# Turning streamed outputs and the last token dims in 32-squares on VectorE, and reading expert 0's slot tables in final order

## The chip, the core and the metric

The kernel runs on one core of a Trainium2 chip. Five engines work side by side, each through its own list of instructions in order: TensorE (PE) multiplies matrices and turns tiles, VectorE (DVE) and ScalarE (ACT) work on elements, GpSimd (POOL) does small element work and issues the indexed transfers, and SyncE (SP) issues the plain transfers. Transfers run on 16 DMA engines that all queues share. SBUF is the on-chip memory of 128 partitions; PE writes its products into PSUM, from where ScalarE or VectorE copies them.

The metric is device time in microseconds, the median of several runs. Lower is better.

## The reference

Two blocks follow one another. Attention: for each of 8 batches x 8 heads, 576 queries against 576 keys of 64 dims; only scores within tau of the row's largest are kept, and the softmax over them weights the values.

```python
scores = scale * np.matmul(q, k.transpose(0, 1, 3, 2))
thresh = np.max(scores, axis=-1, keepdims=True) - tau
scores = np.where(scores >= thresh, scores, -1000000000.0)
scores = scores - np.max(scores, axis=-1, keepdims=True)
attn = np.exp(scores)
attn = attn / (np.sum(attn, axis=-1, keepdims=True) + 1e-09)
return np.matmul(attn, v).astype(np.float32)
```

The heads of a position are put side by side, which gives x, 4608 tokens of 512 dims. Then each token goes through one of 8 experts, chosen by a hash of its id; an expert is two matrices (512 x 1024, 1024 x 512, fp32) with a ReLU between:

```python
expert_idx = token_ids * np.int64(2654435761) % np.int64(E)
for e in range(E):
    mask = expert_idx == e
    xe = x[mask]
    h = np.maximum(xe @ w1[e], 0.0)
    out[mask] = h @ w2[e]
```

## The kernel before

**Attention** (to about 470 us). A loop over 160 steps, five for each of the 32 pairs of heads, in an order written out by hand. A step computes scores on PE, copies them negated with their maximum on VectorE (L227), takes the exponential on ScalarE (L241), masks and sums on VectorE (L252), turns the weights on PE (L263) and copies the turned ones on ScalarE. The normalised output of a pair goes to the scratch tensor x in DRAM (L333, then stores L339 and L344). SP also issues the loads of the next pairs (L169 to L193) and the weights of experts 0 and 1 (L118, L123).

**Routing** runs in pieces between these steps. Every token gets a slot: expert e owns 608 slots. 36 indexed writes put the token numbers into two slot tables in DRAM, by even and odd columns. Eight reads bring the tables back into `stok` and `stok_odd` (L493), a minimum joins them (L498), and copies with a step of 4 put them into the order of token tiles, `gidx` (L512). Four small multiplies make `gidx_0`, the index of each of expert 0's tokens in each quarter of 128 dims (L503). After the loop the same copies are made for the other experts, and `gidx_x`, in the order of 32-squares (L736).

**The hand-over.** Three quarters of expert 0's token dims are gathered while attention still runs (L108), turned on PE into `xT_0`, and multiplied as pieces between the last attention steps (`early_h`, L587, copied by VectorE at L594). The last quarter comes from the last pairs. It is gathered after them, turned by ten half-tile turns on PE (L563), copied by ScalarE (L577) and multiplied in `late_h` (L604); VectorE adds that to the earlier sum (L609) and ScalarE applies the ReLU (L610). The first product of `late_h` goes into a PSUM tile of which there is one, and the third product needs it again. The tiles of the expert stage are laid into the SBUF bytes that the attention stage gives up; VectorE clears five of them and an output tile at the start (L755, L757).

**Experts** (from about 500 us). An expert e has 19 blocks of 32 token slots: three tiles of 128 slots and a rest of 224, called "streamed". PE does, in this order:

- `gemm1` (L773), h = ReLU(w1 x), copied by ScalarE and VectorE in turn;
- `gemm2_last` (L799), the rest's outputs, transposed: the weights w2 are the stationary operand and the 224 slots stream by. ScalarE copies the result to `oT_sb` (L803);
- three times `gemm2` (L787), a tile of 128 slots each. Behind the first and the second stands `turn_last` (L810), four PE turns that bring one tile of the rest back to rows.

Each output tile is copied by ScalarE (L815) and stored by an indexed store on GpSimd to the output rows (L816). Successive stores all write the output tensor, so each waits for the one before. Meanwhile GpSimd gathers the tokens of expert e+2 (`fetch`), VectorE turns those of e+1 in 32-squares (`turn_x`, L831), and 16 moves on SP put the squares in place (L836). SP then loads the weights of e+2. A loop for tokens over an expert's 608 slots ends the program; it has no turn in this data.

Of the kernel before, what the change touches and what calls it, by code (L numbers as in the profile page):

```python
# [20 lines left out]
def kernel(  # L21
# [12 lines left out]
    nc = tc.nc  # L34
# [61 lines left out]
    gidx = consts.tile([P, E, KT], I32, name="gidx")  # L96
    gidx_0 = consts.tile([P, KT, HP], I32, name="gidx_0")
    gidx_x = consts.tile([P, E, KT], I32, name="gidx_x")
    ov_i = consts.tile([P, NOV + 1], I32, name="ov_i")
# [13 lines left out]
    def fetch_0(kt, hp):  # L113
        gather(x_rows, xg_bufs[kt][:, P * hp:P * hp + P], gidx_0[:, kt, hp:hp + 1])

    def load_w1(e):
# [9 lines left out]
    with tc.tile_pool(name="a_q", bufs=1) as a_q, \  # L126
# [353 lines left out]
        def scatters():  # L480
# [8 lines left out]
            for _ in range(4):  # L489
                yield  # L490
            for table, dst in zip(slot_dram, (stok, stok_odd)):
                for h in range(HP):
                    nc.sync.dma_start(  # L493
                        out=dst[32 * h:32 * h + 32],
                        in_=table[0:E * CAP].rearrange("(e c s) o -> c e (s o)", e=E, c=32))
            for _ in range(4):
                yield
            nc.vector.tensor_tensor(out=stok[:], in0=stok[:], in1=stok_odd[:], op=ALU.min)  # L498
            yield
            by_tiles(0, 1)  # L500
            yield
            for h in range(HP):
                nc.vector.tensor_scalar(out=gidx_0[:, :, h], in0=gidx[:, 0], scalar1=float(HP),  # L503
                                        scalar2=float(h), op0=ALU.mult, op1=ALU.add)
                if h == 1:
                    yield
            routed.append(True)

        def by_tiles(e0, e1):
            for h in range(4):  # L510
                rows, n = slice(32 * h, 32 * h + 32), (NB - h + 3) // 4
                nc.vector.tensor_copy(gidx[rows, e0:e1, 0:n], stok[rows, e0:e1, h::4])  # L512

# [30 lines left out]
        def constants():  # L544
# [6 lines left out]
            nc.gpsimd.memset(gidx[:], BIG)  # L551
            nc.gpsimd.memset(gidx_x[:], BIG)
            nc.gpsimd.iota(tok[:], pattern=[[1, NTC]], base=0, channel_multiplier=NTC)
            for table in slot_dram:
# [72 lines left out]
        with tc.manual_schedule():  # L627
# [104 lines left out]
            assert not early  # L732
            by_tiles(1, E)
            for g in range(4):
# [4 lines left out]
            fill(FO * 2 * (CO - 1) - 18)  # L739
            tr = ps_tr.tile([P, 2, 512], FP32, name="tr")  # L740
            early_xT(tr, 0, KT, CO - 1, CO)

    with tc.tile_pool(name="m_x", bufs=1) as m_x, \
# [6 lines left out]

        o_bufs = [m_o.tile([P, DIN], FP32, name=f"o_{i}") for i in range(KT)]
        xg_sets = [xg_bufs, [m_x.tile([P, DIN], FP32, name=f"xh_{i}") for i in range(KT)]]
        xq = m_x.tile([P, DIN // 32, 32 * KT], FP32, name="xq")
        for xg in xg_sets[1]:
            nc.vector.memset(xg[:], 0.0)  # L755
        oT_sb = m_o.tile([P, CO, CAP - FIRST[KF]], FP32, name="oT_sb")
        nc.vector.memset(o_bufs[KT - 1][:], 0.0)  # L757
        mark = m_o.tile([P, 1], FP32, name="mark")

        def put_xT(xg, xT, kt, rows):  # L760
            tr = ps_x.tile([P, 2, 512], FP32, name="xT_ps")[:, 0].rearrange(
                "p (c q) -> p c q", c=CO)
            for co in range(CO):
                nc.tensor.transpose(tr[:, co, 0:rows], xg[0:rows, co * P:co * P + P],
                                    ident[0:rows, 0:rows])
            nc.vector.tensor_copy(xT[:, :, FIRST[kt]:FIRST[kt] + rows], tr[:, :, 0:rows])

# [15 lines left out]

        def gemm2(w2_sb, h_sb, kt, idx, rows):
            o_ps = ps_o.tile([P, DIN], FP32, name="o_ps")
            for fo in range(FO):
                nc.tensor.matmul(o_ps[0:rows], lhsT=h_sb[:, fo, FIRST[kt]:FIRST[kt] + rows],  # L787
                                 rhs=w2_sb[:, fo, :], start=(fo == 0), stop=(fo == FO - 1))
            store(o_ps, kt, idx, rows)

        def gemm2_last(w2_sb, h_sb, order=range(FO)):

            oT_ps = ps_sc.tile([P, 2, 512], FP32, name="sc")
            width = CAP - FIRST[KF]
            for i in range(2):
                for c in range(CO // 2):
                    co = CO // 2 * i + c
                    for fo in order:
                        nc.tensor.matmul(oT_ps[:, i, c * width:c * width + width],  # L799
                                         lhsT=w2_sb[:, fo, co * P:co * P + P],  # L800
                                         rhs=h_sb[:, fo, FIRST[KF]:CAP], start=(fo == order[0]),
                                         stop=(fo == order[-1]))
            nc.scalar.copy(oT_sb[:].rearrange("p (i c) s -> p i (c s)", i=2),  # L803
                           oT_ps[:, :, 0:CO // 2 * width])

        def turn_last(kt, idx):
            o_ps = ps_x.tile([P, 2, 512], FP32, name="xT_ps")[:, 0]
            s0, rows = FIRST[kt] - FIRST[KF], TROWS[kt]
            for co in range(CO):
                nc.tensor.transpose(o_ps[0:rows, co * P:co * P + P], oT_sb[:, co, s0:s0 + rows], ident[:])  # L810
            store(o_ps, kt, idx, rows)

        def store(o_ps, kt, idx, rows):
            o_sb = o_bufs[kt % len(o_bufs)]
            nc.scalar.copy(o_sb[0:rows], o_ps[0:rows])  # L815
            nc.gpsimd.indirect_dma_start(  # L816
                out=out[:, :], out_offset=bass.IndirectOffsetOnAxis(ap=idx, axis=0),
                in_=o_sb[:], in_offset=None, bounds_check=N - 1, oob_is_err=False)

# [7 lines left out]
        def turn_x(e):  # L827


            for k in range(KT):  # L830
                nc.vector.transpose(out=xq[:, :, 32 * k:32 * k + 32],  # L831
                                    in_=xg_sets[e % 2][k][:].rearrange("p (d a) -> p d a", a=32))
            for g in range(4):
                s0, s1 = 32 * KT * g, min(32 * KT * (g + 1), CAP)
                for r in range(4):
                    nc.sync.dma_start(out=xT_bufs[e % 2][32 * r:32 * r + 32, :, s0:s1],  # L836
                                      in_=xq[32 * g:32 * g + 32, r::4, 0:s1 - s0])

        with tc.manual_schedule():
# [4 lines left out]
            for e in range(E):  # L844
# [8 lines left out]
                for kt in range(KF):  # L853
                    gemm2(w2_sb, h_bufs[e % 2], kt, gidx[:, e, kt:kt + 1], P)
                    if kt < KT - KF:
                        turn_last(KF + kt, gidx[:, e, KF + kt:KF + kt + 1])
                    if kt == 0 and e + 2 < E:
                        fetch(e + 2)
# [5 lines left out]
        with tc.For_i(0, n_ov, 1) as it:  # L864
# [15 lines left out]
            gather(x_dram, xg_bufs[0][:], idx[:, 0:1])  # L880
            put_xT(xg_bufs[0], xT_0, 0, P)
            gemm1(w1_sb, xT_0, h_0, 1, P)
            gemm2(w2_sb, h_0, 0, idx[:, 0:1], P)

# [33 lines left out]
```

## Time and profile before

| | us |
|---|---|
| time, median of 3 runs | 1012.16 (1010.39 to 1014.26) |
| profiled execution, time | 1007.16 |
| profiled execution, span | 1005.6 |
| PE busy | 991.6 (99%) |
| VectorE busy | 509.2 (51%) |
| ScalarE busy | 451.4 (45%) |
| GpSimd busy | 292.2 (29%) |
| `gemm2_last` on PE, L799 | 98.2 |
| turns of the streamed outputs on PE, L810, 64 of them | 9.6 |

The table's busy times are those of one profiled execution. PE's granted clock was 0.997 of full speed. Matmul ends in the profile are modelled, so the distance between the starts of two products says more than their lengths. A line of a timeline gives start and length in us, the engine, the line of the kernel, the operation, output and inputs, how many such instructions stand together, and in brackets how long the engine was idle before and for what. "SPq" is the SP queue issuing a transfer. Each fp32 matmul appears twice in the counts.

### The profile page before, as it was taken

The numbers are of one execution on the slowest core, as the hardware profiler recorded it, in microseconds if no ns is written. First come the engines' busy times: TensorE is split into PE (matmuls) and PEld (weight loads), VectorE is DVE, ScalarE is ACT, GpSimd is POOL, SyncE is SP. The second block draws the span as 40 slices with busy tenths as digits, with TensorE's granted clock in tenths as the row PEclk, the third lists the DMA queues.
The fourth block names the chain that finished last, engine by engine and source line by source line (L and its number), as shares of the span: only waits on it lengthen the run. The fifth ranks groups of instructions, "written<-read, shape, count | busy, mean of one in ns | idle before, by whom it ended". The sixth has DMA issues, their size and how long they took to land. (4 is left out here: it accounts for less than half of the span.)

```text
span 1005.6 us, 20293 instructions
## 1 busy us (share of the span) xinstructions
PE 991.6 (99%) x7612; PEld 658.3 (65%) x7612; DVE 509.2 (51%) x1366; ACT 451.4 (45%) x735; POOL 292.2 (29%) x411
## 2 busy tenths in 40 slices
PE   7999999999999999999999999999999999999996
PEld 4666666666666666666766857767678577685783
DVE  7999999999999999994302010010010100100000
ACT  5888889888898888883210010110110100101101
POOL 3233323377776335540413030030210300301001
PEclk9999999999999999999999999999999999999998
DMA  7345544555367757410157234262262432600001
GB/s 179 80 124 141 129 120 111 132 141 119 95 179 180 180 158 189 109 45 24 46 163 215 84 96 133 84 208 73 78 178 84 126 103 93 190 25 32 16 1 48
DMA packets 112002, 113.38 MB, mean 113 GB/s; under 512 B 26340, under 2 KB 86248, under 8 KB 111904
## 3 DMA queue, kind: packets, MB, share of 16 engines
q1 hardware_dynamic: 103680, 92.95, 34.9%
q0 software_dynamic: 7792, 18.91, 6.0%
q8 instruction: 62, 1.02, 0.4%
q14 instruction: 36, 0.29, 0.1%
q10 hardware_dynamic: 432, 0.21, 0.1%
HBM read 81.98 MB, written 22.37 MB: 104 GB/s over the span
## 5 line engine op out<-in xcount | busy, mean ns | idle before, releaser
L241 ACT ACTIVATE w<-ns,nmx 128x576 f32<-128x576 f32 x288 | 220.5, 776 | 36.5 <-DVE ns L227 36.2
L773 PE MATMUL sc<-xT,w_sb 128*128 128x304 f32 x896 | 230.4, 419 | 0.0
L252 DVE SCALAR_TENSOR_TENSOR w<-ns,thr,w 128x576 f32<-128x576 f32 x288 | 226.0, 817 | 0.0
L773 PEld LDWEIGHTS sc<-xT,w_sb 128*128 128x128 f32 x896 | 170.2, 190 | 61.4 <-issue 3.3
L227 DVE TENSOR_SCALAR_CACHE_REDUCE ns<-sc 128x576 f32<-128x576 f32 x288 | 205.6, 746 | 5.5 <-PE sc L216 4.5
L216 PE MATMUL sc<-k_sb,q 64*128 64x288 f32 (+1 forms) x1280 | 179.7, 425 | 1.6 <-DVE k_sb L541 0.9
L787 PE MATMUL o_ps<-w_sb,h 128*128 128x512 f32 x384 | 168.7, 592 | 0.0
L263 PEld LDWEIGHTS tr<-ident,w 64*128 64x128 f32 x2624 | 106.3, 138 | 88.6 <-ACT wT_b L284 26.3
L816 POOL DMA_INDIRECT out_dram<-o,gidx x40 | 39.5, 989 | 415.9 <-ACT o L815 320.4
L234 POOL TENSOR_SCALAR thr<-nmx,drop 128x2 f32<-128x2 f32 (+1 forms) x160 | 102.2, 639 | 174.8 <-DVE ns L227 162.1
L263 PE MATMUL tr<-ident,w 64*128 64x64 f32 x2624 | 139.0, 230 | 2.7 <-ACT wT_a L284 2.0
L781 DVE TENSOR_SCALAR h<-sc 128x608 f32<-128x608 f32 x28 | 22.2, 792 | 234.0 <-PE sc L773 234.0
L787 PEld LDWEIGHTS o_ps<-w_sb,h 128*128 128x128 f32 x384 | 71.7, 190 | 80.4 <-issue 80.4
L216 PEld LDWEIGHTS sc<-k_sb,q 64*128 64x128 f32 (+1 forms) x1280 | 92.9, 178 | 24.9 <-DVE ns L227 11.1
L779 ACT ACTIVATE h<-sc 128x608 f32<-128x608 f32 x28 | 19.0, 677 | 182.0 <-PE sc L773 182.0
L294 PE MATMUL av<-wT_a,v 128*64 128x320 f32 (+1 forms) x704 | 100.4, 418 | 0.0
L799 PE MATMUL sc<-h,w_sb 128*128 128x224 f32 x512 | 98.2, 352 | 0.0
L799 PEld LDWEIGHTS sc<-h,w_sb 128*128 128x128 f32 x512 | 96.9, 190 | 1.1
L284 ACT COPY wT_a<-tr 128x512 f32<-128x512 f32 (+1 forms) x128 | 81.8, 639 | 20.1 <-PE tr L263 19.6
L284 ACT COPY wT_b<-tr 128x512 f32<-128x512 f32 (+1 forms) x128 | 81.3, 635 | 5.4 <-PE tr L263 3.2
L294 PE MATMUL av<-wT_b,v 128*64 128x256 f32 x640 | 83.2, 389 | 0.0
L815 ACT COPY o<-o_ps 128x512 f32<-128x512 f32 x24 | 14.1, 586 | 147.3 <-issue 87.3
(114 smaller groups left out, 559.4 us busy)
## 6 DMA issues: line engine op xcount, KB each, us to landing
w_sb<-in_moe_w_dram SPq DMA_DIRECT2D x16, 2048.0 KB
q<-in_q_dram SPq DMA_DIRECT2D x62, 288.0 KB
v<-in_v_dram SPq DMA_DIRECT2D x32, 256.0 KB
x_scratch<-xm SPq DMA_DIRECT2D x32, 256.0 KB
xT<-xq SPq DMA_DIRECT2D x84, 80.0 KB
k_sb<-in_k_dram SPq DMA_DIRECT2D x31, 144.0 KB
k_sb<-in_k_dram SPq DMA_DIRECT2D x32, 112.0 KB
x_scratch<-xg SPq DMA_DIRECT2D x9, 256.0 KB
```

Of the source, the lines that this page charges most:

```text
L216: nc.tensor.matmul(sc[out_rows, i, 0:S2], lhsT=q_sb[rows, h, q0:q1], rhs=k_sb[rows, h], start=True, stop=True)
L227: nc.vector.tensor_scalar(out=ns[:].rearrange("p (i s) -> p i s", i=2), in0=sc[:, :, 0:S2], scalar1=-1.0, scalar2=None, op0=ALU.mult, op1= ...
L234: nc.gpsimd.tensor_scalar(out=thr[:, 0:j + 1], in0=stats[n][0][:, 0:j + 1], scalar1=drop[:], scalar2=None, op0=ALU.add)
L241: nc.scalar.activation(w, nss[n, j][:], AF.Exp, bias=stats[n][0][:, j:j + 1], scale=-1.0)
L252: nc.vector.scalar_tensor_tensor(out=w, in0=nss.pop((n, j))[:], scalar=stats[n][1][:, j:j + 1], in1=w, op0=ALU.is_le, op1=ALU.mult, accum_ ...
L263: nc.tensor.transpose(dst[:, r, 64 * c:64 * c + 64], src[rows, c0:c0 + P], ident[rows, rows])
L284: nc.scalar.copy(dst, tr[:, :, 0:64 * n_c].rearrange("p r (c q) -> p r c q", c=n_c))
L294: nc.tensor.matmul(av[64 * j:64 * j + 64, g, c0:c1], lhsT=v_sb[:, c, 64 * j:64 * j + 64], rhs=wT[g][:, i, c0:c1], start=(c == 0), stop=stop)
L773: nc.tensor.matmul(h_ps[:, i, 0:width], lhsT=w1_sb[:, co, fo * P:fo * P + P], rhs=xT[:, co, i * width:i * width + width], start=(co == 0), ...
L787: nc.tensor.matmul(o_ps[0:rows], lhsT=h_sb[:, fo, FIRST[kt]:FIRST[kt] + rows], rhs=w2_sb[:, fo, :], start=(fo == 0), stop=(fo == FO - 1))
L799: nc.tensor.matmul(oT_ps[:, i, c * width:c * width + width], lhsT=w2_sb[:, fo, co * P:co * P + P], rhs=h_sb[:, fo, FIRST[KF]:CAP], start=( ...
L816: nc.gpsimd.indirect_dma_start(out=out[:, :], out_offset=bass.IndirectOffsetOnAxis(ap=idx, axis=0), in_=o_sb[:], in_offset=None, bounds_ch ...
```

## The change

Three edits. Lines are those of the kernel before.

1. The streamed outputs are no longer copied by ScalarE and turned by PE. `gemm2_last` takes every fourth column of w2 as its stationary operand, so that partition p holds output dims 4p to 4p+3. VectorE turns the result in squares of 32 x 32 out of PSUM into `oq`, two instructions an expert, and 16 moves on SP put the squares into rows in `o_last`. The two stores of these rows follow the store of the second product.
2. The last quarter of expert 0's token dims is turned in 32-squares too: five turns on VectorE into the bytes of an attention buffer, then 16 moves on SP into `xT_0`. Its gathers use the slot order that this needs.
3. Expert 0's slots are read from the tables by 16 small transfers of their own, in the two orders in which they are used (`sidx`), ahead of the eight reads of the whole tables. One minimum and two multiply-adds make `gidx_0` from them. The minimum and the copies over the whole tables move behind the attention loop.

```diff
+    def move_squares(xq, xT, c0):
+        for g in range(4):
+            s0, s1 = 32 * KT * g, min(32 * KT * (g + 1), CAP)
+            for r in range(4):
+                nc.sync.dma_start(out=xT[32 * r:32 * r + 32, c0:CO, s0:s1],
+                                  in_=xq[32 * g:32 * g + 32, r::4, 0:s1 - s0])
...
+            for table, dst in zip(slot_dram, sidx):
+                slots = table[0:CAP].rearrange("(c s) o -> c (s o)", c=32)
+                for h in range(4):
+                    for part in range(2):
+                        blocks = (slots[:, h::4] if part == 0 else
+                                  slots[:, KT * h:min(KT * h + KT, NB)])
+                        nc.sync.dma_start(
+                            out=dst[32 * h:32 * h + 32, part, 0:blocks.shape[1]], in_=blocks)
             for table, dst in zip(slot_dram, (stok, stok_odd)):
...
-            nc.vector.tensor_tensor(out=stok[:], in0=stok[:], in1=stok_odd[:], op=ALU.min)
-            yield
-            by_tiles(0, 1)
-            yield
-            for h in range(HP):
-                nc.vector.tensor_scalar(out=gidx_0[:, :, h], in0=gidx[:, 0], scalar1=float(HP),
-                                        scalar2=float(h), op0=ALU.mult, op1=ALU.add)
-                if h == 1:
-                    yield
+            nc.vector.tensor_tensor(out=gidx_e[:], in0=sidx[0][:], in1=sidx[1][:], op=ALU.min)
+            yield
+            for part, h0, h1 in ((0, 0, HP - 1), (1, HP - 1, HP)):
+                nc.vector.scalar_tensor_tensor(
+                    out=gidx_0[:, :, h0:h1],
+                    in0=gidx_e[:, part, :, None].to_broadcast([P, KT, h1 - h0]),
+                    scalar=float(HP), in1=iota_i[:, None, h0:h1].to_broadcast([P, KT, h1 - h0]),
+                    op0=ALU.mult, op1=ALU.add)
+                yield
...
+            for t in sidx:
+                nc.gpsimd.memset(t[:], BIG)
...
-            by_tiles(1, E)
+            nc.vector.tensor_tensor(out=stok[:], in0=stok[:], in1=stok_odd[:], op=ALU.min)
+            for h in range(4):
+                rows, n = slice(32 * h, 32 * h + 32), (NB - h + 3) // 4
+                nc.vector.tensor_copy(gidx[rows, :, 0:n], stok[rows, :, h::4])
...
             fill(FO * 2 * (CO - 1) - 18)
-            tr = ps_tr.tile([P, 2, 512], FP32, name="tr")
-            early_xT(tr, 0, KT, CO - 1, CO)
+            xq_0 = w_bufs[0][:, 0:P // 32 * 32 * KT].rearrange("p (d s) -> p d s", d=P // 32)
+            for kt in range(KT):
+                nc.vector.transpose(
+                    out=xq_0[:, :, 32 * kt:32 * kt + 32],
+                    in_=xg_bufs[kt][:, DIN - P:DIN].rearrange("p (d a) -> p d a", a=32))
+            move_squares(xq_0, xT_0, CO - 1)
...
-        oT_sb = m_o.tile([P, CO, CAP - FIRST[KF]], FP32, name="oT_sb")
-        nc.vector.memset(o_bufs[KT - 1][:], 0.0)
+        oq = m_o.tile([P, NB - 4 * KF, 32, CO], FP32, name="oq")
+        o_last = m_o.tile([P, KT - KF, DIN], FP32, name="o_last")
+        nc.vector.memset(o_last[:], 0.0)
...
-                                         lhsT=w2_sb[:, fo, co * P:co * P + P],
+                                         lhsT=w2_sb[:, fo, co::CO],
                                          rhs=h_sb[:, fo, FIRST[KF]:CAP], start=(fo == order[0]),
                                          stop=(fo == order[-1]))
-            nc.scalar.copy(oT_sb[:].rearrange("p (i c) s -> p i (c s)", i=2),
-                           oT_ps[:, :, 0:CO // 2 * width])
-
-        def turn_last(kt, idx):
-            o_ps = ps_x.tile([P, 2, 512], FP32, name="xT_ps")[:, 0]
-            s0, rows = FIRST[kt] - FIRST[KF], TROWS[kt]
-            for co in range(CO):
-                nc.tensor.transpose(o_ps[0:rows, co * P:co * P + P], oT_sb[:, co, s0:s0 + rows], ident[:])
-            store(o_ps, kt, idx, rows)
+            for i in range(2):
+                cols = slice(CO // 2 * i, CO // 2 * i + CO // 2)
+                nc.vector.transpose(
+                    out=oq[:, :, :, cols].rearrange("p b a c -> p c b a"),
+                    in_=oT_ps[:, i, 0:CO // 2 * width].rearrange("p (c b s) -> p c b s", b=width // 32,
+                                                                 s=32))
+            for h in range(4):
+                n = (NB - h + 3) // 4 - KF
+                for g in range(4):
+                    nc.sync.dma_start(
+                        out=o_last[32 * h:32 * h + 32, 0:n, P * g:P * g + P],
+                        in_=oq[32 * g:32 * g + 32, h::4].rearrange("p b a c -> p b (a c)"))
...
                 for kt in range(KF):
-                    gemm2(w2_sb, h_bufs[e % 2], kt, gidx[:, e, kt:kt + 1], P)
-                    if kt < KT - KF:
-                        turn_last(KF + kt, gidx[:, e, KF + kt:KF + kt + 1])
+                    gemm2(w2_sb, h_bufs[e % 2], kt, gidx[:, e, kt:kt + 1])
+                    if kt == 1:
+                        for k in range(KF, KT):
+                            put_rows(o_last[:, k - KF], gidx[:, e, k:k + 1])
                     if kt == 0 and e + 2 < E:
                         fetch(e + 2)
```

`put_rows` is the indexed store that stood in `store`; `turn_x` calls `move_squares` for its own 16 moves. The loop for surplus tokens takes the shortened calls, with no other change.

## The prediction, made before the changed kernel ran

> **What bounds the kernel now.** I read the engine totals first, then busy time by stretch, then the groups of the expert stage, and last the timelines of the hand-over and of the end. In the stretches below, the columns are busy time on PE, PE weight loads, VectorE, ScalarE and GpSimd, then clock, DMA share and GB/s. In the attention stage (30 to 330 us) PE and VectorE are both full, VectorE with 298.5 of 300 us; in the expert stage (from 500 us) PE alone is full, with 47.5 us of VectorE and 72.4 us of GpSimd in 505.
>
> ```profile
> 30.00:330.00 300.00, 299.84 (x3741) 188.66 (x3736) 298.53 (x844) 263.27 (x430) 143.32 (x207) 1.00 0.53 132
> 500.00:1005.00 505.00, 497.76 (x1856) 345.69 (x1854) 47.54 (x64) 49.01 (x78) 72.42 (x75) 0.99 0.34 102
> ```
>
> So an instruction taken from VectorE counts before 470 us, one taken from PE counts after it. The groups that the change touches (mean ns last before the idle time):
>
> ```profile
> L799 PE MATMUL sc<-h,w_sb 128*128 128x224 f32 x512 | 98.2, 352 | 0.0
> L799 PEld LDWEIGHTS sc<-h,w_sb 128*128 128x128 f32 x512 | 96.9, 190 | 1.1
> L831 DVE STREAM_TRANSPOSE xq<-xh 128x512 f32<-128x512 f32 x20 | 14.1, 709 | 94.0 <-DMA xh<-x_scratch,gidx_x 94.0
> L512 DVE COPY gidx<-stok 32x35 int32<-32x35 int32 x3 | 0.6, 197 | 0.0
> L736 DVE COPY gidx_x<-stok 32x35 int32<-32x35 int32 x3 | 0.5, 178 | 0.0
> ```
>
> What the PE turns of L810 really cost is read from the starts of one expert's three products (timeline, start and length):
>
> ```profile
> 578.13 7.03 PE L787 MATMUL o_ps<-w_sb,h 128*128 128x512 f32 x16
> 585.44 7.03 PE L787 MATMUL o_ps<-w_sb,h 128*128 128x512 f32 x16
> 592.74 7.03 PE L787 MATMUL o_ps<-w_sb,h 128*128 128x512 f32 x16
> 599.61 0.68 PE L773 MATMUL sc<-xT,w_sb 128*128 128x304 f32 x2
> ```
>
> With four turns behind it a product takes 7.31 and 7.30 us, without them 6.87: a turn of four costs 0.43 us, though its busy time is 0.60.
>
> The hand-over from attention to experts, in order of time:
>
> ```profile
> 482.07 1.01 POOL L108 DMA_INDIRECT xg<-x_scratch,gidx  x1 [0.30 <-issue]
> 484.44 0.79 DVE L594 COPY h<-sc 128x608 f32<-128x608 f32 x1 [2.28 <-PE sc L587]
> 488.43 0.69 PE L563 MATMUL tr<-ident,xg 64*128 64x64 f32 x10
> 491.20 1.19 PE L604 MATMUL xT_ps<-xT,w_sb 128*128 128x304 f32 x4
> 492.48 0.79 DVE L609 TENSOR_TENSOR h<-h,xT_ps 128x608 f32<-128x608 f32 x1 [7.25 <-PE xT_ps L604]
> 493.33 1.29 PE L604 MATMUL xT_ps<-xT,w_sb 128*128 128x304 f32 x4
> 506.00 10.40 SPq L836 DMA_DIRECT2D xT<-xq  x16
> ```
>
> PE turns the last token dims at 488.42 with the gathers already there, and never stands still. The last line prices what will replace those turns: SP takes 10.40 us to issue 16 moves.
>
> The end, output stores of the last expert on GpSimd (the third left out):
>
> ```profile
> 984.09 0.98 POOL L816 DMA_INDIRECT out_dram<-o,gidx  x1 [50.74 <-ACT o L815]
> 987.84 0.98 POOL L816 DMA_INDIRECT out_dram<-o,gidx  x1 [2.77 <-issue]
> ...
> 994.85 0.98 POOL L816 DMA_INDIRECT out_dram<-o,gidx  x1 [2.48 <-DMA out_dram<-o,gidx]
> 998.71 0.98 POOL L816 DMA_INDIRECT out_dram<-o,gidx  x1 [2.88 <-ACTq L864]
> ```
>
> Each store waits until the one ahead has landed (2.68 us in the chain of waits), so two cannot start less than 3.45 to 3.75 us apart.
>
> **What the Trainium skill says.** "DMA: Bandwidth & Descriptors", section "Anatomy of one DMA", gives about 2.0 us fixed per DMA, most of it the receipt of the write; here a store of x whose issue ended at 474.62 let a gather start at 476.71, which agrees. "SBUF — State Buffer", section "Door 1: The DMA port swizzle", says that lines are 16 bytes and an access that moves to a new line each time pays, while fp32 strides up to 4 may be free: it leaves exactly this change's stride open. "TensorE: Matmul & The Clock Gate", section "LDWEIGHTS", prices a load at columns/1.2, 107 ns for 128; the trace shows 190 ns for one and has no strided one.
>
> **The change part by part.**
>
> *Slot tables.* In attention VectorE loses one minimum (its followers start 0.27 us later for it), four copies (0.72 us with the gap) and four small multiplies (two pairs at 0.14): 1.27 us. It gains a minimum over 10 columns and two multiply-adds, about 0.12 us each by the L503 starts: 0.36. Sum -0.9 us, on the bounding engine. The big minimum and copies now run near 473 us, where VectorE has 6.4 of 19 us of work. SP gets 16 reads more at 334 us, 0.48 to 0.65 us each: 7.7 to 10.4 us, less 2.3 idle. Queued behind them: the next pair's loads (issued 340.3 to 343.6), then values, the x stores and an expert's weights. Those keys then land near 353 at worst; GpSimd scales them at 361.06. Cost nothing; without that cover up to 8 us. Two GpSimd memsets at the start, 0.13 us each, lie in its 0.56 us idle before L234.
>
> *Expert 0's last dims.* PE loses ten turns, 488.42 to 489.05: 0.63 us. What is late next is the first L604 product, which now waits for moves. The last gather lands 482.07 + 3.3 = 485.4; VectorE's copy ends at 485.23; five squares of 128 columns: from 709 ns for 512, some 0.2 us each in a row, so 486.3. Then 16 moves on SP. At the cadence of L836 they take 10.4, at that of the stok reads (four in 1.92 us) 7.7; I take 9.7 (0.37 for the first, 0.62 for each other): 496.1. Landing 1.9 later: 498.0. The second half of the first product needs all moves; before, it started 0.52 after 491.20, at 491.7. So 6.4 us later. Second, the memsets of L755 and L757: in before they ran early, in the shadow. In the order of the changed kernel the first one waits for all these moves, since its tile takes over the bytes of the buffer they read, and stands ahead of L609 on VectorE. Five at 0.52 and one of 1024 columns at 1.0: 3.6 us, to 501.65. L609's add then ends at 502.5, and PE's third product, which needs its PSUM tile, starts there and not at 493.33: **+9.2 us** in all (7 to 10.5 with both cadences, and landing 1.5 to 2.5). The fetches of expert 1, its squares and moves shift along; their slack is 14 us (moves done 518.5, used at 533.3).
>
> *Streamed outputs.* PE loses 16 turns of four at 0.43: 6.9 us, of which the 14 of experts 0 to 6 are sure: **-6.0 us**. ScalarE loses 3 copies an expert, off the path. VectorE gains two transposes of 448 columns, about 0.7 us each, up to 1.3 with the strided write; SP 16 moves, 9.7 us. From 978 they land by about 991, three us ahead of their store's turn, so hidden; without cover each us late is a us only for the last expert. Ahead of them on SP stands the weight load of expert e+2, ten us, done by then except for expert 0, where nothing but stores waits.
>
> *The end.* The two o_last stores now follow product 2's store, ahead of product 3's. Product 2's output is copied by 983.82 + 6.87 = 990.69, stored at 990.96; three chained gaps of 3.6 put the last store at 1001.7, against 998.71: **+3.0 us** (2.6 to 3.5) for expert 7, whose own 0.87 us of PE gain is lost too. In the other experts the same queue-up delays only stores: behind it on GpSimd stands the next expert's first store, some 30 us on.
>
> Sum: -0.9 + 9.2 - 6.0 + 3.0 = +5.3 us. Against its own execution (span 1005.6, time 1007.16) this gives 1012.5; the median of the runs is 5.0 above that one, 1012.16, so the forecast is 1017.5.
>
> *Weights read with a step of CO.* L799 now loads each column 16 bytes from the next, 512 times. Matmuls come every 98.2/512 = 192 ns, so a load is hidden up to about that. Floor: nothing. Ceiling, by the DVE's L434, whose 288 elements at 144-byte steps took 684 ns where L470's 256 contiguous took 408, about 1.8 times per element: 107 becomes 193 to 214 and costs up to 25 ns x 512 = 13 us; if the whole 190 doubles, 97 us. L512 against L736, the same shape with and without a 16-byte step, 197 against 178 ns, speaks for a mild price: I take nothing.
>
> **Rivals.** *Strided weights show:* the place is the 12.27 us of L799 per expert; it decides from about 190 ns of real load time on. +13 us on top: 1030; in a doubled case 1115. For it: loads fill 96.9 of 98.2 us. Against it: the same 190 ns stands in L773, where the slot is 257 ns, so it includes latency. *Not slower:* SP issues the hand-over's moves at 0.37 us, as first ones after a pause do, because they are a quarter as large as those of L836: 16 x 0.41 = 6.6 us and 1.5 to land put PE's wait 3.6 lower, +1.7 in all, 1013.9. It decides where the sixteen take under 9.4 us. For it: no row of that shape. Against it: L193's 16 KB moves take 0.57 each too. *The change does not do what it says:* excluded, the compiled order of the changed kernel has no turn of L810 left.
>
> **How the numbers follow.** Forecast 0.55 (own range 1014.5 to 1021), strided weights 0.27 (a third of it above 1032), not slower 0.18. What a measurement can tell from no change is 0.5%, 5 us: the forecast lies just above it, so of its 0.55 some 0.31 is slower and 0.24 same; of the last case 0.14 is same and 0.04 faster. Slower 0.58, same 0.38, faster 0.04. The range 1013 to 1032 leaves out a few hundredths below and the dear end of the strided loads.
>
> **What would show it.** Right: PE idle some 7 us near 491 and 3 more behind L609; product starts 6.87 apart; last store chained three deep; L799 still 12.2 us. Wrong: L799 longer, sixteen moves under 8 us, memsets clear of the moves, or a pair near 355 us longer than 13.9.

## The result, and the profile after

The changed kernel takes 1040.97 us (median of 6 runs, 1039.99 to 1042.04); the kernel before took 1011.92 beside it (6 runs, 1010.39 to 1014.26). The ratio is 1.0285, with an interval from 1.0271 to 1.0299: slower by 29 us. The forecast was slower, but by 5 us, and its range ended at 1032. Every ratio in this document is to runs of the kernel before taken beside it; on the chips of the experiments below these took 1012.05, 1007.74 and 1007.48 us. Line numbers from here on are those of the kernel named.

The busy times by stretch, in the same columns as before (PE, PE weight loads, VectorE, ScalarE, GpSimd, clock, DMA share, GB/s), for the changed kernel:

```profile
30.00:330.00 300.00, 298.68 (x3698) 186.34 (x3698) 295.68 (x836) 260.39 (x425) 139.55 (x206) 1.00 0.52 131
512.00:1038.00 526.00, 515.41 (x1801) 364.02 (x1799) 63.35 (x82) 35.82 (x56) 73.75 (x76) 0.99 0.35 105
```

The bounds are the ones of before: VectorE and PE together in attention, PE alone in the expert stage. So the time must be in PE's own work there, or in its waits. The groups on the page of the changed kernel show the first:

```profile
L826 PEld LDWEIGHTS sc<-h,w_sb 128*128 128x128 f32 x512 | 120.3, 329 | 0.5
L826 PE MATMUL sc<-h,w_sb 128*128 128x224 f32 x512 | 120.4, 396 | 0.0
L832 DVE STREAM_TRANSPOSE oq<-sc 128x448 f32<-128x448 f32 x16 | 14.2, 963 | 107.5 <-PE sc L826 107.5
```

L826 is `gemm2_last`, L799 of before. One weight load, 190 ns before, takes 329; the 512 products (as the profile counts them, two for each fp32 matmul) took 98.2 us before and take 120.4. They are the same in number, in columns streamed and in type. Only the weights' addresses differ, each column 16 bytes from the next. VectorE's new squares (L832) take 963 ns each, inside the 1.3 us allowed for the strided write, and stand off the path.

The hand-over on the changed kernel's timeline (start, length, then engine, line, operation; idle time before it in brackets):

```profile
488.75 1.08 DVE L761 STREAM_TRANSPOSE w<-xg 128x128 f32<-128x128 f32 x5
489.86 10.08 SPq L123 DMA_DIRECT2D xT<-w  x16
496.32 0.75 PE L620 MATMUL xT_ps<-xT,w_sb 128*128 128x304 f32 x2 [2.29 <-DMA xT<-w]
501.37 1.35 PE L620 MATMUL xT_ps<-xT,w_sb 128*128 128x304 f32 x2 [4.30 <-DMA xT<-w]
501.49 2.65 DVE L778 MEMSET xh<- 128x512 f32 x5 [11.65 <-DMA xT<-w]
505.12 0.73 DVE L625 TENSOR_TENSOR h<-h,xT_ps 128x608 f32<-128x608 f32 x1
505.91 2.39 PE L620 MATMUL xT_ps<-xT,w_sb 128*128 128x304 f32 x4 [1.16 <-DVE h L625]
514.12 15.05 PE L826 MATMUL sc<-h,w_sb 128*128 128x224 f32 x64
```

Sixteen moves go out in 10.08 us, PE pauses 2.29 and 4.30 us for them, the memsets wait for them and hold up the add of L625, and the third product waits for the add. One thing was in no forecast: two products of 304 columns took 0.75 us at 496.32 and 1.35 us at 501.37. The stretches of the changed kernel around that point (the number after GpSimd's is the granted clock) say what went with it:

```profile
496.00:501.00 5.00, 0.75 (x2) 0.30 (x2) 0.00 (x0) 0.00 (x0) 0.00 (x0) 0.84 0.12 30
501.00:506.00 5.00, 3.47 (x7) 1.94 (x7) 3.98 (x7) 0.11 (x1) 0.00 (x0) 0.50 0.00 0
506.00:509.00 3.00, 3.00 (x6) 2.09 (x7) 0.66 (x1) 1.16 (x2) 1.21 (x2) 0.50 0.00 0
509.00:512.00 3.00, 3.00 (x12) 2.13 (x11) 0.91 (x2) 1.44 (x3) 1.21 (x2) 0.89 0.30 86
```

From 501 to 509 the granted clock is 0.50; in the third stretch PE is never idle and gets 6 products done, in the fourth 12. The clock had fallen earlier, near 499.4, inside the pause: 0.84 over the 5 us from 496 leaves 1.6 us at 0.50.

The end on the changed kernel's timeline, the last expert's three products in a row (48 instructions) and its last four stores:

```profile
1006.65 20.76 PE L810 MATMUL o_ps<-w_sb,h 128*128 128x512 f32 x48
1021.48 0.98 POOL L844 DMA_INDIRECT out_dram<-o,gidx  x1 [5.89 <-ACT o L813]
1024.44 0.98 POOL L844 DMA_INDIRECT out_dram<-o_last,gidx  x1 [1.98 <-DMA out_dram<-o,gidx]
1027.40 0.98 POOL L844 DMA_INDIRECT out_dram<-o_last,gidx  x1 [1.98 <-DMA out_dram<-o_last,gidx]
1031.63 0.98 POOL L844 DMA_INDIRECT out_dram<-o,gidx  x1 [3.25 <-DMA out_dram<-o_last,gidx]
```

The two stores of `o_last` stand in a chain between the second product's store and the third's, 2.96, 2.96 and 4.23 us apart.

Put together, between marks that both traces have (us, one profiled execution each):

| stretch | before | after | difference |
|---|---|---|---|
| start of the span to the last op on `xm`, attention's end | 472.21 | 475.70 | +3.5 |
| from there to expert 0's first product of `gemm2_last` | 27.48 | 38.42 | +10.9 |
| `gemm2_last`, all experts | 98.2 | 120.4 | +22.2 |
| rest of the expert stage, to PE's end (997.76; 1027.41) | 399.87 | 392.89 | -7.0 |
| PE's end to the start of the last store | 0.95 | 4.22 | +3.3 |
| from there to the end of the span | 6.89 | 6.67 | -0.2 |
| span | 1005.6 | 1038.3 | +32.7 |

The medians differ by 29.05, not by 32.7: the profiled execution of before (1007.16) lies 4.8 us below its median, that of the changed kernel (1040.11) 0.9 below. The first row is such scatter as well: the same mark lies at 474.82, 472.37 and 471.33 in three experiments below that leave all of attention as before, on one chip, and at 472.42, 471.49 and 470.57 in three that have attention as changed.

### The profile page after: what moved, and what is told of

Its sections match the earlier page's. It is cut to its first block, busy times and chain, and to the rows that moved or that the text cites. A ratio compares the mean times of both kernels' runs of the same rounds, so it can differ in the third digit from the quotient of the medians.

```text
span 1038.3 us, 20349 instructions
## 1 busy us (share of the span) xinstructions
PE 1011.3 (97%) x7538; PEld 675.2 (65%) x7538; DVE 524.8 (51%) x1382; ACT 436.0 (42%) x707; POOL 289.5 (28%) x413
## 5 line engine op out<-in xcount | busy, mean ns | idle before, releaser
L810 PE MATMUL o_ps<-w_sb,h 128*128 128x512 f32 x384 | 166.1, 592 | 0.0
L804 DVE TENSOR_SCALAR h<-sc 128x608 f32<-128x608 f32 x28 | 22.2, 792 | 241.2 <-PE sc L796 241.2
L844 POOL DMA_INDIRECT out_dram<-o,gidx x24 | 23.9, 997 | 390.3 <-ACT o L813 342.9
L826 PEld LDWEIGHTS sc<-h,w_sb 128*128 128x128 f32 x512 | 120.3, 329 | 0.5
L826 PE MATMUL sc<-h,w_sb 128*128 128x224 f32 x512 | 120.4, 396 | 0.0
```

What stands on the lines that cost most here:

```text
L810: nc.tensor.matmul(o_ps[:], lhsT=h_sb[:, fo, FIRST[kt]:FIRST[kt] + P], rhs=w2_sb[:, fo, :], start=(fo == 0), stop=(fo == FO - 1))
L826: nc.tensor.matmul(oT_ps[:, i, c * width:c * width + width], lhsT=w2_sb[:, fo, co::CO], rhs=h_sb[:, fo, FIRST[KF]:CAP], start=(fo == order ...
L844: nc.gpsimd.indirect_dma_start(out=out[:, :], out_offset=bass.IndirectOffsetOnAxis(ap=idx, axis=0), in_=o_sb, in_offset=None, bounds_check ...
```

## The experiments

The theory after the result: the stride of the weights costs about 22 us, the hand-over about 11, the end about 3, and the turns give back 7. The first rival was that the stride is innocent and the loads are long because of the new traffic around them, the moves and squares. Others were that the hand-over's loss is the memsets, not the moves, and that the slot tables moved something.

### The changed kernel without the stride

```diff
-                                         lhsT=w2_sb[:, fo, co::CO],
+                                         lhsT=w2_sb[:, fo, co * P:co * P + P],
```

> The changed kernel with one edit: the stationary operand of gemm2_last is 128 contiguous columns of w2 again, not every fourth. The streamed rows then come out with their output dims in another order; all other instructions are those of the changed kernel. Theory (the step of 16 bytes makes the weight load the limit): the 512 products of this line fall from 235 to 192 ns apart, their busy time from 120.4 to about 98.2 us, and the time by 22 us, to about 1019. Rival (the products are slowed by what runs beside them now, the squares on VectorE and the moves on SP, or by PE's clock): the line stays near 120 us and the time near 1041. The wait at the hand-over and the chained stores at the end stay as they are under both.

Measured: 1018.85 us, ratio to before 1.006 (1.004 to 1.0081). On its page:

```profile
L826 PEld LDWEIGHTS sc<-h,w_sb 128*128 128x128 f32 x512 | 96.9, 190 | 1.1
L826 PE MATMUL sc<-h,w_sb 128*128 128x224 f32 x512 | 98.2, 352 | 0.0
```

All moves and squares are still there and the load is back at 190 ns. The stride is worth 1040.97 - 1018.85 = 22.1 us, and what is left is +6.8 us (4.0 to 8.2 by the interval), where the forecast's likeliest case had +5.3.

### The kernel before with the stride alone, and with two others

The same operand in the kernel before, with a step of 4 elements (16 bytes), of 2 (8 bytes) and of 8 (32 bytes). Nothing else of the change is in these.

```diff
-                                         lhsT=w2_sb[:, fo, co * P:co * P + P],
+                                         lhsT=w2_sb[:, fo, co::CO],
```

> The kernel before with one edit: the stationary operand of gemm2_last takes every fourth column of w2, 16 bytes apart. The streamed rows then hold their output dims in another order; PE still turns them, everything else is the kernel before. Theory (the step alone slows the weight load, with no squares and no moves beside it): L799 takes 120.4 and not 98.2 us, a load shows 329 and not 190 ns, the time rises by 22 us to about 1034. Rival (the load is slow only beside the changed kernel's moves and squares): L799 stays at 98.2, the time at 1012.

```diff
+                                         lhsT=w2_sb[:, fo, co // 2 * 2 * P + co % 2:co // 2 * 2 * P + 2 * P:2],
```

> As the run with a step of four, but every second column, 8 bytes apart, so that two columns share 16 bytes; the order of the streamed output dims is again another one. Theory (what costs is a new 16-byte line for every column): L799 stays at 98.2 us and a load at 190 ns, the time at 1012. Rival (any step costs): the load lies between 190 and 329 ns, and L799 rises where it passes the room that a product of 224 columns leaves.

```diff
+                                         lhsT=w2_sb[:].rearrange("p f d -> p (f d)")[
+                                             :, fo // 2 * 2 * DIN + 4 * (fo % 2) + co:fo // 2 * 2 * DIN + 2 * DIN:8],
```

> As the run with a step of four, but every eighth column of two neighbouring rows of w2, 32 bytes apart; the streamed outputs are then not those of the reference (wrong pairs of weights and hidden units), with the same instructions and shapes. Theory (a new line for every column costs once, however far away it is): like the step of four, a load 329 ns, L799 120.4 us, the time 1034. Rival (the cost grows with the distance): a load of 400 ns or more, L799 above 140 us.

Step of 16 bytes, its groups:

```profile
L799 PE MATMUL sc<-h,w_sb 128*128 128x224 f32 x512 | 120.4, 396 | 0.0
L799 PEld LDWEIGHTS sc<-h,w_sb 128*128 128x128 f32 x512 | 120.3, 329 | 0.5
```

Step of 8 bytes:

```profile
L799 PE MATMUL sc<-h,w_sb 128*128 128x224 f32 x512 | 98.2, 353 | 0.0
L799 PEld LDWEIGHTS sc<-h,w_sb 128*128 128x128 f32 x512 | 97.0, 197 | 1.0
```

Step of 32 bytes:

```profile
L799 PE MATMUL sc<-h,w_sb 128*128 128x224 f32 x512 | 122.9, 401 | 0.0
L799 PEld LDWEIGHTS sc<-h,w_sb 128*128 128x128 f32 x512 | 122.8, 335 | 0.5
```

Times beside a before of 1007.74: 1030.39 (ratio 1.0221, 1.0204 to 1.0238) for 16 bytes, and a single run each, so without an interval, for 8 bytes (1007.65) and 32 bytes (1031.43). With 16 bytes the kernel before loses 22.65 us and shows the very 120.4 us of the changed kernel: the traffic rival has fallen. The price is a step and no slope: by the busy times 8 bytes cost nothing, 16 cost 43 ns a product (120.4 less 98.2, by 512), and 32 only 5 more (122.9 less 120.4, by 512). Nothing between 8 and 16 bytes was run.

### The hand-over turned on PE again

```diff
-            xq_0 = w_bufs[0][:, 0:P // 32 * 32 * KT].rearrange("p (d s) -> p d s", d=P // 32)
-            for kt in range(KT):
...
-            move_squares(xq_0, xT_0, CO - 1)
+            tr = ps_tr.tile([P, 2, 512], FP32, name="tr")
+            early_xT(tr, 0, KT, CO - 1, CO)
```

The index of the last quarter then uses the tables' other order (`part` 0), as it must.

> The changed kernel with expert 0's last token dims turned on PE again, by the ten half-tile turns and ScalarE copies of the kernel before; streamed outputs and slot tables as changed. Theory (the hand-over costs 11 us: the wait for 16 moves, the memsets behind it, and slow products after the wait): the first streamed product of expert 0 starts about 11 us earlier than in the changed kernel, the products of late_h take 9.6 us again and not 13.4, and the time falls by 11 us to about 1030. Rival (the late start comes from the attention stage, which ended 3.5 us later in the changed kernel's profile): at most 7 us are won.

Measured: 1029.73, ratio 1.0169 (1.0149 to 1.0189), 11.2 us under the changed kernel. On its timeline, the first product of the last quarter and the first streamed one:

```profile
495.43 1.19 PE L620 MATMUL xT_ps<-xT,w_sb 128*128 128x304 f32 x4
503.94 15.05 PE L822 MATMUL sc<-h,w_sb 128*128 128x224 f32 x64
```

From one to the other 8.5 us, as before (491.20 to 499.69); in the changed kernel 17.8 (from 496.32). The stretch itself shows what the time shows. Attention ended at 476.44 here, no earlier than in the changed kernel (475.70), so the rival, a late start that comes from attention, falls.

### The memsets clear of the moves

The squares go into a tile of their own, so that clearing the expert stage's tiles has no move to wait for.

```diff
-            xq_0 = w_bufs[0][:, 0:P // 32 * 32 * KT].rearrange("p (d s) -> p d s", d=P // 32)
+    xq_0 = consts.tile([P, P // 32, 32 * KT], FP32, name="xq_0")
```

> The changed kernel with the squares of expert 0's last dims in an SBUF tile of their own, so that the tiles cleared by the memsets no longer take over bytes that the moves read; everything else as changed. Theory (the memsets stand behind the moves and ahead of the first add on VectorE, and the third product of late_h waits for that add): the memsets run near 475 us, the first add follows the first product at once, and about 3 us are won: 1038. Rival (only the landing of the moves counts, the memsets run beside products that PE has to do anyway): under 1 us.

Measured: 1038.82, ratio 1.0269 (1.0249 to 1.0289), 2.2 us under the changed kernel. On its timeline:

```profile
473.87 1.02 DVE L778 MEMSET xh<- 128x512 f32 x2 [4.12 <-PE av L305]
...
501.25 1.35 PE L621 MATMUL xT_ps<-xT,w_sb 128*128 128x304 f32 x2 [4.30 <-DMA xT<-xq]
...
504.43 1.98 PE L621 MATMUL xT_ps<-xT,w_sb 128*128 128x304 f32 x4
```

The memsets now run 28 us earlier, and the wait of 4.30 us for the moves stands as it was. The third product starts 3.18 us after the second half of the first, where the changed kernel has 4.54, and the streamed product 7.06 us after that, where it has 8.21. So the traces put the memsets at 2.5 us, 1.36 before the third product and 1.15 behind it; the expectation had about 3. The memsets are the smaller part; the moves are the larger.

### The sixteen moves on two queues

```diff
-                nc.sync.dma_start(out=xT[32 * r:32 * r + 32, c0:CO, s0:s1],
-                                  in_=xq[32 * g:32 * g + 32, r::4, 0:s1 - s0])
+                engines[r % len(engines)].dma_start(
+                    out=xT[32 * r:32 * r + 32, c0:CO, s0:s1],
+                    in_=xq[32 * g:32 * g + 32, r::4, 0:s1 - s0])
...
-            move_squares(xq_0, xT_0, CO - 1)
+            move_squares(xq_0, xT_0, CO - 1, (nc.sync, nc.scalar))
```

> The changed kernel with the 16 moves of the hand-over issued half on SP's queue and half on ScalarE's. Theory (the wait is made by the cadence of one queue, 16 at 0.63 us): the last move is issued after 5 and not 10 us, the second product of late_h starts about 5 us earlier, and with the shorter pause PE's products after it are less slowed: 5 to 6 us won, about 1035.5. Rival (the wait is made by how long a move takes to land, or by the DMA engines): less than 2 us.

Measured: 1034.73, ratio 1.0227 (1.0208 to 1.0247), 6.2 us under the changed kernel. On its timeline:

```profile
488.21 5.02 SPq L123 DMA_DIRECT2D xT<-w  x8
488.21 5.35 ACTq L123 DMA_DIRECT2D xT<-w  x8
...
495.15 0.75 PE L621 MATMUL xT_ps<-xT,w_sb 128*128 128x304 f32 x2 [1.84 <-DMA xT<-w]
...
499.65 2.29 PE L621 MATMUL xT_ps<-xT,w_sb 128*128 128x304 f32 x4 [2.73 <-DVE h L626]
```

And its stretches:

```profile
495.00:500.00 5.00, 2.13 (x7) 1.41 (x8) 3.98 (x7) 0.38 (x1) 0.00 (x0) 0.98 0.00 0
500.00:505.00 5.00, 5.00 (x14) 3.40 (x14) 1.07 (x2) 2.29 (x4) 1.95 (x4) 0.68 0.20 52
```

The moves' bytes are the same and the issue takes half as long: what the hand-over waited for was the queue that issues, not the transfers. PE's second wait goes from 4.30 to 1.84 us, and the two products behind it run at full speed (0.75 us for both, where they took 1.35). The memsets still stand ahead of the add, so PE pauses 2.73 us before the third product, and then the clock falls here too: 0.98 and 0.68 leave 0.2 and 3.2 us at 0.50.

### The last expert turned by PE, contiguous weights for all

The turned squares are kept for experts 0 to 6 only, with weights read contiguously; the squares then land in 28 moves an expert on two queues. Expert 7 uses the copy and the PE turns of before.

```diff
-                                         lhsT=w2_sb[:, fo, co::CO],
+                                         lhsT=w2_sb[:, fo, co * P:co * P + P],
...
-        oq = m_o.tile([P, NB - 4 * KF, 32, CO], FP32, name="oq")
+        oq = m_o.tile([P, NB - 4 * KF, CO, 32], FP32, name="oq")
...
+                    for k in range(n):
+                        (nc.sync, nc.scalar)[g % 2].dma_start(
+                            out=o_last[32 * h:32 * h + 32, k].rearrange("p (c d) -> p c d", c=CO)[
+                                :, :, 32 * g:32 * g + 32],
+                            in_=oq[32 * g:32 * g + 32, h + 4 * k])
...
+                    if e == E - 1 and kt < KT - KF:
+                        turn_last(KF + kt, gidx[:, e, KF + kt:KF + kt + 1])
```

> The changed kernel with two edits. Contiguous weights with the output dims in their right places: VectorE writes the squares in another order, and 28 moves instead of 16, half of them on ScalarE's queue, put them there. And the last expert's streamed tiles turned by PE as in the kernel before. Theory (the two stores added behind product 2 of the last expert cost 4.2 us between the end of the last product and the last store, against about 1 before, and turning on PE costs 0.9): against the run with contiguous weights alone 2.4 us are won, to about 1016.5, and the last store starts about 1 us after the last product ends. Rival (the end is set by something else, the stores are covered): no gain, or a loss of 0.9.

Measured: 1013.05 beside a before of 1007.74, ratio 1.0051 (1.0034 to 1.0069). On its timeline, the last expert's streamed products and the last two stores:

```profile
969.46 12.27 PE L828 MATMUL sc<-h,w_sb 128*128 128x224 f32 x64
...
1000.30 0.98 POOL L861 DMA_INDIRECT out_dram<-o_last,gidx  x1 [2.48 <-DMA out_dram<-o,gidx]
1004.15 0.98 POOL L861 DMA_INDIRECT out_dram<-o,gidx  x1 [2.87 <-ACT o L815]
```

The last store again waits for its own copy and not for the store ahead. From the start of the last streamed products to the last store it is 34.69 us, as before (964.02 to 998.71); without the stride alone (the first experiment) it was 37.07, 974.10 to 1011.17. So by these two traces the end costs 2.4 us net of expert 7's shorter PE work. The times say less: +5.3 us over before (3.4 to 7.0 by the interval) against +6.8 (4.0 to 8.2) in the first experiment is 1.5 us, from two chips and with ranges that overlap, and the order of the squares and the number of moves changed too. The squares, written contiguously, take less:

```profile
L838 DVE STREAM_TRANSPOSE oq<-sc 128x448 f32<-128x448 f32 x14 | 8.3, 628 | 73.7 <-PE sc L828 73.7
```

### The slot tables alone

The kernel before with the third edit only (all four quarters of expert 0's index take the order that the PE turns need).

```diff
-            nc.vector.tensor_tensor(out=stok[:], in0=stok[:], in1=stok_odd[:], op=ALU.min)
...
+            nc.vector.tensor_tensor(out=gidx_e[:], in0=sidx[0][:], in1=sidx[1][:], op=ALU.min)
```

> The kernel before with the slot-table edit alone: expert 0's slots read by 16 transfers of their own, one minimum and two multiply-adds for gidx_0, the big minimum behind the loop. Theory (VectorE is the bound of the attention stage and loses 1.27 us for 0.36): 0.9 us faster, 0.1%, to be seen in the pair of heads in which the copies stood (14.7 us between two L333 before, about 13.9 now). Rival (the 16 reads hold back the next pair's loads on SP): that pair or the next is longer than 14.7 us, and the time 1 us or more above before.

Measured, over 13 runs beside 17 of before: 1007.18 against 1007.48, ratio 1.0002 (0.9994 to 1.0010), which is not the quotient of the two medians. The change is between -0.6 and +1.0 us, so the forecast -0.9 is not in the time. It is in the trace: the pair in which the edit lies (from one op on `xm` to the next) took 13.92 us here and in the changed kernel, 14.67 before (343.37 to 358.04). Behind the pair nothing is lost: from its end to attention's last op on `xm` it is 114.05 us here and 114.17 before. The pair began 0.49 us later here than before (343.86 and 343.37), no more than single executions differ by. Why the times show no gain stays open.

### What is best of it

The slot tables read as changed, squares and contiguous weights for experts 0 to 6, expert 7 and the hand-over turned by PE: the edits of "The last expert turned by PE" and "The hand-over turned on PE again" on the changed kernel.

> What the runs so far speak for: the slot tables as changed; streamed outputs of experts 0 to 6 turned by VectorE from contiguous weights, 28 moves on two queues; the last expert and the hand-over turned by PE as in the kernel before. Theory (the parts add up): 14 turns of four at 0.44 us saved, 6.1 us, and 0.9 from the slot tables, with nothing else on the path: 7 us below before, ratio 0.993. Rival (the squares or their moves hold something up in every expert, which the larger losses hid): same as before or above.

And the same with the hand-over left to VectorE, but its squares in a tile of their own and its moves on two queues:

> As the run before, but with the hand-over in 32-squares, eased: own tile for the squares, moves on two queues. Theory: the hand-over then still costs some 3 us more than PE's turns (first product after the last move at about 8 us behind the squares, a short pause of PE, no memsets in the way), so 3 to 4 us below before, ratio 0.9965. Rival (with two queues and the tile the wait is fully covered): as fast as the version with PE's turns.

Measured beside a before of 1007.48: 1001.37 for the first, ratio 0.9938 (0.9924 to 0.9952), and 1003.02 for the second, 0.9954 (0.9941 to 0.9968). Both beat the kernel before; the first, by 6.1 us (4.8 to 7.7), is the fastest found. That is the streamed turns' forecast gain of 6.0, whole, once stride, hand-over and end no longer spend it, with nothing to be seen of the slot tables' 0.9. In the second, the timeline and the stretch after it:

```profile
491.64 0.75 PE L622 MATMUL xT_ps<-xT,w_sb 128*128 128x304 f32 x2 [1.81 <-DMA xT<-xq]
```

```profile
493.00:498.00 5.00, 5.00 (x21) 3.55 (x20) 2.12 (x4) 3.09 (x5) 2.40 (x4) 1.00 0.19 52
```

With a wait of 1.81 us the clock stays at 1.00, and the hand-over in squares is only 1.65 us dearer than on PE by the medians, with intervals that overlap.

## Why the prediction was wrong, point by point

**The step that failed** is "Weights read with a step of CO", at "I take nothing". The runs showed 22.2 us (trace), 22.1 and 22.65 (times), of the 29 in all: that the change is slower came true mostly by a term that the likeliest case put at nothing. The choice rested on a VectorE copy whose 16-byte step had cost 19 ns; that is another engine reading, and here it told nothing of PE's loads. The ceiling beside it, "up to 25 ns x 512 = 13 us", was too low as well: it let the products come 193 to 214 ns apart, and they came 235 apart. Its working has two slips: 684 ns for 288 elements against 408 for 256 is 1.5 times per element, not 1.8, and 214 less 192 is 22 ns or 11 us, not 25 and 13. The other end, 97 us, took the whole longer load as visible. Neither is how the two combine: the load got 139 ns longer and the products 43 ns further apart. In both dear cases the distance lies 94 to 95 ns under the load's recorded length (329 and 235, 335 and 240), and in the cheap ones the load less 95 is well below the 192 ns that the product sets itself. So a load's record seems to overlap its neighbours' by some 95 ns; that is read from two points and not shown by a run of its own. The rival "strided weights show" named the right place and the right mechanism, at 0.27 and 1030; with 22 instead of 13 it would have stood at 1039.7.

The Trainium skill bore on this more than the prediction used. The section of "SBUF — State Buffer" that the prediction took to leave the stride open also asks for at least two accesses to a 16-byte line for full speed. A step of 8 bytes has two to a line and one of 16 bytes has one, and the loads of 197 and 329 ns agree with that sentence, not with the one that lets fp32 stride by 4 for free. "GPSIMD Engine Reference", section "Performance pitfalls for Q7 kernels", says of GpSimd that reading SBUF with a step above 8 bytes costs about half more per element. The page speaks of that engine alone, but what the runs show for PE's loads fits it: 8 bytes free, 16 dear. That lines are the reason is not shown by these runs.

**Hand-over, +9.2.** Right in its parts, short in its sum. Measured from attention's end, the second half of the first product came 6.2 us later (6.4 forecast) and the third product 9.1 us later (9.2 forecast). Two misses cancel in the first of these: the sixteen moves took 10.08 us to issue (9.7 forecast), and the product started 1.4 us after the last issue (1.9 forecast). The 2.0 us that the prediction has from "DMA: Bandwidth & Descriptors" is given there for transfers that GpSimd issues; these are SP's. The memsets are 2.2 us of the hand-over by the time of the kernel that has them clear of the moves; the forecast had 9.2 less 6.4, 2.8.

What was not in the sum is behind the third product: from it to the first streamed one it takes 8.21 us instead of 6.36. PE's clock is at 0.50 there until 509.7 (0.89 over the 3 us from 509 leaves 0.66 us), which is 3.8 us from the third product's start, and half of 3.8 is the whole of the 1.85 us. The same sum comes out in four other traces, worked out and measured: squares in their own tile 0.8 and 0.70 us, two queues 1.7 and 1.69, without the stride 2.4 and 2.40, last expert on PE 2.3 and 2.29. That term makes the hand-over 10.9 in the trace and 11.2 in the times. The forecast held a pause of some 7 us and never asked what PE does after one.

"TensorE: Matmul & The Clock Gate", section "What's actually happening", gives both states, half clock after an idle window of about 3.4 us and full clock after a busy one, and says that these windows run freely, whatever the kernel does. The lengths agree: half clock lasts 10.2 us in the changed kernel and 6.8, 3.4, 13.7 and 13.7 us in the four traces just named, which is three, two, one, four and four times 3.41. The pause can be shorter than a window: the clock fell behind one of 2.29 us without the stride and one of 2.73 with two queues, held through the same 2.29 us in the changed kernel, and stayed at 1.00 after 1.84 and 1.81. Nor was the window free of work: the 3.4 us up to the fall at 499.4 hold 0.75 us of products. How much work keeps the clock up is not shown, and how many windows a run loses is in part chance. The rival "not slower", moves at 0.41 us, is refuted: they took 0.63.

**Streamed turns, -6.0.** Right: -7.0 in the trace with all 16 turns, 0.87 of which the forecast put to the last expert, and 6.1 us in the best kernel with 14. Products start 6.87 apart, as said.

**The end, +3.0.** Right in kind, near by luck: +3.3 us from PE's end to the last store, +2.4 when expert 7's gain of 0.87 is set against it, where the forecast had +3.0 after both. The gaps were 2.96, 2.96 and 4.23, not 3.6 each, so two stores can start closer than the 3.45 us that the prediction took as the least; two short gaps and a long one nearly average out. What sets a gap stays open.

**Slot tables, -0.9.** The pair got 0.75 us shorter, the time did not. The cover named for SP's sixteen reads held: the reads took 8.24 us, the next keys were loaded from 348.22 on instead of 340.31, and no wait above 0.2 us followed on VectorE up to 372 us.

**The sum.** Without the stride the likeliest case gave 1017.5 with a range of its own to 1021, and the kernel without the stride took 1018.85. The parts were not each so near: the hand-over came out 1.7 us and the slot tables 0.9 above their terms, the end 0.6 below. What took the forecast out of its range is the one term put at nothing.

## What to carry to other kernels

A layout that saves turns may move its cost into the operand that is read most: here 16 groups of PE turns, worth 7 us, were bought with 512 weight loads at a 16-byte step, 22 us. Where no trace has such a price, neither another engine's row nor nothing may stand for it in a forecast: take the dear value or keep the operand contiguous and permute on the side that is written once. When a bounding engine gets a new wait, count what it waits for by its issue (16 small moves are 10 us on one queue and 5 on two), and count the half-speed time behind a pause: 2.3 us were enough in one trace here, and the loss was 0.7 to 2.4 us.

## What the runs showed of the hardware that was not expected

- A load of 128 x 128 fp32 weights (as recorded, two to a matmul): 190 ns contiguous, 197 with an 8-byte step, 329 with 16 bytes, 335 with 32. Products of 224 columns stand 192, 192, 235 and 240 ns apart with them.
- PE's half clock at the hand-over lasted 3.4, 6.8, 10.2 or 13.7 us in five traces, always a multiple of 3.41. It followed pauses of 2.29, 2.73 or 4.30 us, and none followed pauses of 1.84 and 1.81. The same pause of 2.29 us brought it on in one kernel and not in another.
- Sixteen moves within SBUF took 10.08 us to issue on one queue, and 5.02 and 5.35 us side by side on two.
- A 32-square turn of 448 fp32 columns from PSUM takes 628 ns when it writes rows of 32 and 963 when each element lands 16 bytes from the last.
